# One fixed period per head, evenly spread weight and FFN pieces, and early heads turned by TensorE, in a routed-attention and FFN kernel

## The chip, the cores and the metric

The kernel runs on one core of a Trainium2 chip. The metric is the device time in microseconds (us) from start to end of one execution; lower is better. Engines: TensorE (matmuls and transposes, PE in the profile, its weight loads PEld), VectorE (DVE), ScalarE (ACT), GpSimd (POOL), SyncE (SP, which here only issues DMAs). Before: 346.12 us median of four runs.

Runs carry a state, fast or slow; where a granted TensorE clock is lower and a run over 1.5% above the fastest of its kernel it is called slow. Ratios and their intervals use fast runs alone; medians are of all runs of a kernel, slow ones too.

## The reference

Four batches of eight heads, 768 tokens, head size 64. Each query and key is assigned to the nearest of 16 centroids of its head; attention is allowed only within equal clusters. The heads are joined to 3072 tokens of 512 and go through a multiplicative FFN.

```python
q_assign = argmax(q_n @ c_n);  k_assign = argmax(k_n @ c_n)      # per head, 16 clusters
scores = 0.125 * q @ k.T, masked to -1e9 where q_assign != k_assign
attn = softmax(scores) @ v                                       # 32 heads
x = heads joined: (3072, 512)
a = x @ w1; b = x @ w2                                           # 512 -> 1024
out = ((a * b) @ w3) @ w_out                                     # 1024 -> 1024 -> 512
```

## The kernel before

Per head g the kernel does: three loads (192 KB each); *prep* on POOL (bf16 copy and the rounding rest of q and k into `stg`, v into `vb`); a *turn* of `stg` into `xqk` by a DMA transpose, so that the head size lies on partitions; *routing* (12 small matmuls into `prr`, three VectorE operations to a one-hot `oh`, a transpose into `pso`, one more VectorE operation to `ohT`, then four small DMAs that write the one-hot rows into rows 64-79 of `xqk`, where they act as the mask); *scores* and exponentials; *values* (36 matmuls into `av`), normalising, and after every second head a join into `xT_all`. Beside that, w3 and w_out are folded once into one matrix `wc` (16 pieces), and each block of 512 tokens needs 12 FFN pieces (8 up, 4 down). Six blocks exist; a block can start when its batch of eight heads is done, so two blocks always remain for a tail after the last head.

The loop, shortened:

```python
LOAD_AHEAD = 4; PREP_AHEAD = 3; ROUTE_AHEAD = 2
for g in range(NG + 1):                       # 32 heads; the scheduler orders the engines
    if g < NG:
        stage_load(g + 4); stage_prep(g + 3)  # prep ends with the DMA transpose
        emit_wloads(2)
        stage_route(g + 2)
        stage_sc(g)
    if g >= 1:
        stage_av(g - 1)
        ...                                   # a batch done: its FFN units go to pending
    for _ in range(UNITS(g)):                 # 2 for g < 8, else 3, as long as there are some
        if pending: pending.pop(0)()

def stage_prep(g):
    ...
    nc.sync.dma_start_transpose(out=xqk, in_=stg)        # all 32 heads
```

An up unit is eight matmuls 128x512 (two groups of four, then a ScalarE copy and a VectorE product), a down unit eight more.

The softmax here doesn't subtract the row's maximum and nothing guards it: scores larger than these inputs give would overflow.

## Time and profile before

| | before |
|---|---|
| time, median of 4 | 346.12 us (344.51 to 347.29) |
| profiled span, mean granted clock | 348.0 us, 0.978 |
| TensorE busy | 287.2 us, 83% |
| first score matmul | 36.5 us |
| last head's FFN tail | from 302.6 us, 45 us with the end |

The page of the kernel before. The first lines are the busy time of each engine with its share of the span; each digit below is the busy share in a fortieth of the span, in tenths (9 is 90% or more). PEclk is the granted TensorE clock.

```profile
span 348.0 us, 7211 instructions
PE 287.2 (83%) x2818; PEld 171.6 (49%) x2818; DVE 159.4 (46%) x316; ACT 184.3 (53%) x351; POOL 102.3 (29%) x112
...
PE   0120748888999999879698989998999999799995
PEclk9999969899999999999899999999999999999999
DMA  7999799768798633697493474444502320001103
```

TensorE does little in the first four slices (35 us) while DMA stands at 7 to 9. It also dips to 8, 7 and 6 in the 17th, 18th and 20th slices, long after the start. The profiled run took 350.15 us, 4 us more than the median.

The same kernel cut into stages, busy time of each engine by stretch. Columns: the stretch and its length, busy us of each engine with its instruction count, then granted clock, share of DMA engines busy, GB/s.

```profile
0.00:36.50 36.50, 5.09 (x62) 3.71 (x62) 12.28 (x43) 2.77 (x3) 19.15 (x27) 1.00 0.98 213
36.50:105.00 68.50, 58.49 (x649) 38.51 (x650) 35.27 (x67) 41.71 (x80) 31.28 (x33) 0.93 0.87 179
105.00:140.00 35.00, 33.31 (x305) 18.92 (x304) 17.12 (x30) 20.03 (x39) 12.40 (x13) 1.00 0.56 140
140.00:173.00 33.00, 27.42 (x367) 18.79 (x364) 15.70 (x35) 25.76 (x51) 14.46 (x15) 0.95 0.70 145
173.00:244.50 71.50, 66.10 (x632) 37.82 (x630) 38.28 (x65) 40.94 (x78) 20.99 (x22) 1.00 0.56 137
244.50:282.50 38.00, 37.76 (x361) 22.40 (x360) 17.80 (x37) 23.65 (x46) 3.99 (x5) 1.00 0.31 79
282.50:302.60 20.10, 18.71 (x267) 13.31 (x264) 8.56 (x21) 17.78 (x36) 0.00 (x0) 1.00 0.07 21
302.60:348.00 45.40, 40.33 (x189) 18.18 (x189) 14.38 (x21) 11.60 (x20) 0.00 (x0) 0.98 0.12 47
```

Only 5 of the first 36.5 us are TensorE work, with the DMA engines 98% busy. The fourth row is heads 12-15, which have no FFN piece left. The last row is the tail.

What TensorE waited for, before: engine, tile and line, releaser, total us, number of waits, longest.

```profile
PE prr L267 <- DMA xqk<-stg: 17.2, 4, 6.7
PE sc L299 <- DMA xqk<-ohT: 10.2, 4, 3.7
PE pct L162 <- DVE cnsrc L156: 8.2, 1, 8.2
PE pt L175 <- DMA w3b<-in_moe_w_dram: 5.7, 2, 3.9
```

The routing matmuls wait for turned heads (`xqk<-stg`), the scores for one-hot rows (`xqk<-ohT`).

### The profile page before, as it was taken

How to read it: one execution, taken by the hardware profiler on the slowest of the kernel's cores; microseconds unless marked ns; L12 is line 12 of the kernel's file. 1: busy time of each engine (PE TensorE's matmuls, PEld its weight loads, DVE VectorE, ACT ScalarE, POOL GpSimd, SP SyncE). 2: the span in 40 equal slices, each digit the busy share in tenths (PEclk: the TensorE clock that was granted, in tenths of full speed). 3: DMA queues.
4: the chain of work that ended last, by engine and by line, in shares of the span. 5: the costliest groups of instructions: out<-in, count | busy, mean ns of one | idle time of the engine just before them, and what ended most of it. 6: DMA issues, size and time to landing. Idle time of an engine off the chain costs nothing.

```text
span 348.0 us, 7211 instructions
## 1 busy us (share of the span) xinstructions
PE 287.2 (83%) x2818; PEld 171.6 (49%) x2818; DVE 159.4 (46%) x316; ACT 184.3 (53%) x351; POOL 102.3 (29%) x112
## 2 busy tenths in 40 slices
PE   0120748888999999879698989998999999799995
PEld 0120536555655555657355555554656556544442
DVE  7222425465555544555256556544555444342331
ACT  3000438756565656779546555655676659532230
POOL 3960434426554522343533332312300000000000
PEclk9999969899999999999899999999999999999999
DMA  7999799768798633697493474444502320001103
GB/s 204 244 183 223 142 210 150 191 134 178 198 231 185 185 86 106 178 164 153 88 236 95 132 207 119 119 99 75 163 21 48 81 97 10 2 0 58 66 0 121
DMA packets 74961, 45.07 MB, mean 129 GB/s; under 512 B 54448, under 2 KB 69808, under 8 KB 74928
## 3 DMA queue, kind: packets, MB, share of 16 engines
q1 hardware_dynamic: 71696, 39.37, 47.0%
q0 software_dynamic: 3232, 5.24, 9.0%
q8 instruction: 22, 0.36, 0.4%
q14 instruction: 11, 0.09, 0.1%
HBM read 29.39 MB, written 6.29 MB: 103 GB/s over the span
## 4 chain that ended last, share of the span: by engine, by line
PE 65%; DMA 14%; DVE 11%; POOL 3%; SPq 2%; ACT 2%; issue 2%; DVEq 0%; POOLq 0%; ACTq 0%
PE po L232 12%; PE pb L220 12%; PE pa L212 12%; PE sc L299 9%; PE av L322 7%; DMA xqk<-stg 5%; PE sc L305 5%; PE pw L186 4%; DMA x_273<-in_v_dram 4%; PE pso L281 2%; DMA xqk<-ohT 2%; DMA x_113<-in_v_dram 2%; DVE rsc L269 2%; DVE oh_139 L273 2%; PE prr L267 2%
## 5 line engine op out<-in xcount | busy, mean ns | idle before, releaser
L302 ACT ACTIVATE ex<-sc 128x512 bf16<-128x512 f32 x192 | 107.2, 621 | 68.0 <-PE sc L299 67.6
L299 PE MATMUL sc<-xqk 80*128 80x512 bf16 x192 | 71.5, 396 | 11.6 <-DMA xqk<-ohT 10.2
L322 PEld LDWEIGHTS <-ex 128*128 128x128 bf16 x1152 | 63.2, 99 | 22.3 <-issue 5.6
L309 ACT ACTIVATE ex<-sc 128x512 bf16<-128x512 f32 x96 | 60.4, 630 | 11.6 <-PE sc L305 11.5
L217 ACT CAST asb<-pa 128x512 bf16<-128x512 f32 x48 | 27.8, 586 | 47.0 <-PE pa L212 46.9
L212 PE MATMUL pa<-xT_all,w1b 128*128 128x512 bf16 x192 | 52.0, 381 | 0.6 <-DVE xT_all L344 0.6
L220 PE MATMUL pb<-xT_all,w2b 128*128 128x512 bf16 x192 | 52.0, 380 | 0.2 <-ACT asb L217 0.2
L224 DVE TENSOR_TENSOR ab<-pb,asb 128x512 bf16<-128x512 f32 x48 | 33.2, 691 | 41.0 <-PE pb L220 35.6
L232 PE MATMUL po<-wc,ab 128*128 128x512 bf16 x192 | 43.1, 379 | 0.0
L305 PE MATMUL sc<-xqk 80*128 80x256 bf16 x192 | 38.8, 280 | 0.0
L269 DVE TENSOR_REDUCE rsc<-prr 128x192 f32<-128x384 f32 x32 | 17.6, 551 | 33.8 <-PE prr L267 33.8
L267 PE MATMUL prr<-cnt_189,xqk 128*128 128x32 bf16 x384 | 15.4, 178 | 17.7 <-DMA xqk<-stg 17.2
L232 PEld LDWEIGHTS <-ab 128*128 128x128 bf16 x192 | 18.5, 98 | 21.7
L220 PEld LDWEIGHTS <-w2b 128*128 128x128 bf16 x192 | 18.6, 98 | 21.5 <-issue 1.6
L267 PEld LDWEIGHTS <-xqk 128*128 128x128 bf16 x384 | 14.7, 98 | 25.8 <-DMA xqk<-stg 19.0
L212 PEld LDWEIGHTS <-w1b 128*128 128x128 bf16 x192 | 18.1, 98 | 19.0 <-issue 0.3
L283 DVE TENSOR_SCALAR ohT<-pso,msc 128x384 bf16<-128x384 bf16 x32 | 15.2, 476 | 19.3 <-PE pso L281 15.1
L299 PEld LDWEIGHTS <-xqk 80*128 80x128 bf16 x192 | 17.4, 100 | 12.7 <-DMA xqk<-ohT 11.7
L240 ACT COPY osb<-po 128x512 f32<-128x512 f32 x12 | 7.0, 585 | 28.5 <-PE po L232 28.5
L330 DVE RECIPROCAL rcp<-av 128x6 f32<-128x6 f32 x32 | 6.3, 196 | 33.7 <-PE av L322 33.3
L238 DVE COPY osb<-po 128x512 f32<-128x512 f32 x12 | 8.3, 691 | 26.0 <-PE po L232 26.0
L305 PEld LDWEIGHTS <-xqk 80*128 80x128 bf16 x192 | 16.3, 100 | 6.6 <-issue 0.8
(167 smaller groups left out, 330.3 us busy)
## 6 DMA issues: line engine op xcount, KB each, us to landing
out_dram<-osb SPq DMA_DIRECT2D x24, 256.0 KB, 2.2
w3b<-in_moe_w_dram POOLq DMA_DIRECT2D x4, 512.0 KB, 7.2
xqk<-ohT SPq DMA_DIRECT2D x128, 12.0 KB, 1.8
wob<-in_moe_w_out_dram POOLq DMA_DIRECT2D x2, 512.0 KB, 11.5
w1b<-in_moe_w_dram POOLq DMA_DIRECT2D x2, 512.0 KB, 5.4
w2b<-in_moe_w_dram POOLq DMA_DIRECT2D x2, 512.0 KB, 8.4
xqk<-stg SPq DMA_TRANSPOSE x32, 4.2
x_105<-in_q_dram SPq DMA_DIRECT2D x1, 192.0 KB, 2.4
```

Of the source, the lines that this page charges most:

```text
L212: nc.tensor.matmul(pa, lhsT=w1b[:, fc, js], rhs=xT_all[:, fc, t0 : t0 + TB], start=(fc == 0), stop=(fc == 3),)
L217: nc.scalar.copy(out=asb, in_=pa)
L220: nc.tensor.matmul(pb, lhsT=w2b[:, fc, js], rhs=xT_all[:, fc, t0 : t0 + TB], start=(fc == 0), stop=(fc == 3),)
L224: nc.vector.tensor_tensor(out=st["ab"][:, jc], in0=pb, in1=asb, op=ALU.mult)
L232: nc.tensor.matmul(po, lhsT=st["ab"][:, jc, sub * P : (sub + 1) * P], rhs=wc[:, jc], start=(jc == 0), stop=(jc == 7),)
L267: nc.tensor.matmul(prr[:, j], lhsT=xqk[:, j, :], rhs=cnt2[:, h], start=True, stop=True)
L269: nc.vector.tensor_reduce(out=rsc, in_=prr, axis=AX.X, op=ALU.add)
L299: nc.tensor.matmul(sc, lhsT=xqk[0:KR, NCH + 2 * pr + i, :], rhs=xqk[0:KR, 0:4, :], start=True, stop=True)
L302: nc.scalar.activation(out=ex[:, i, 0:512], in_=sc, func=ACT.Exp, scale=SM_SCALE)
L305: nc.tensor.matmul(sc[:, i], lhsT=xqk[0:KR, NCH + 2 * pr + i, :], rhs=xqk[0:KR, 4:6, :], start=True, stop=True,)
L309: nc.scalar.activation(out=ex[:, :, 512:S], in_=sc, func=ACT.Exp, scale=SM_SCALE)
L322: nc.tensor.matmul(av[:, sub, 0:VCOL], lhsT=exs[j // 2][:, j % 2, sub * P : (sub + 1) * P], rhs=vb[:, j, 0:VCOL], start=(j == 0), stop=(j ...
```

## The change

Its intent: make the start short and keep TensorE evenly loaded. All engines get the program's own order (no scheduler). There is one period per head; each item in it has a position between 0 and 1, and items are emitted in order of position. Weight and FFN units become half pieces (at most four matmuls 128x512; a fold turn is eight transposes). Heads 0-9 are turned by TensorE transposes through PSUM. Two heads are loaded first instead of four, head 0 is prepared on VectorE, weights are issued one or two per period. Routing leads the scores by one period instead of two. Two smaller things changed with it: a fold turn now needs only one quarter of w3 to have landed instead of all of it, and there are seven buffers for exponentials instead of eight.

```diff
-LOAD_AHEAD = 4
-PREP_AHEAD = 3
-ROUTE_AHEAD = 2
+PE_HEADS = 10
...
+    def turn_pe(g: int, half: int):
+        def item():
...
+            pst = psum_f.tile([P, NCH, P], BF16, name="pst", tag="f")
+            for j in range(NCH):
+                nc.tensor.transpose(out=pst[:, j], in_=st["stg"][:, half * NCH + j], identity=ident)
+            nc.vector.tensor_copy(out=st["xqk"][:, half * NCH : (half + 1) * NCH], in_=pst)
...
+    LOADS = {-2: [2], -1: [3], 0: [4], 1: [5], 2: [6], 3: [7, 8], 4: [9, 10]}
...
+    def in_period(p: int):
+        for g in LOADS.get(p, []):
+            load(g)
+        if PE_HEADS <= p + 3 < NG:
+            turn_dma(p + 3)
...                                            # prep, on POOL
+        wload()
+        if p >= 2:
+            wload()
+        work = []
+        if 0 <= p < NG:
+            work += [((i + 0.5) / 9, it) for i, it in enumerate(score_items(p))]
+        if 0 <= p + 2 < PE_HEADS:
+            work += [(0.50, turn_pe(p + 2, 0)), (0.62, turn_pe(p + 2, 1))]
+        if 0 <= p + 1 < NG:
+            work += [(0.02, route(p + 1)), (0.36, route_turn(p + 1))]
+        if 1 <= p <= NG:
+            work += [(0.23 + 0.13 * i, it) for i, it in enumerate(av_items(p - 1))]
...
+        n = FILL(p, len(fill))
+        for i in range(min(n, len(fill))):
+            work.append(((i + 0.75) / n, fill.pop(0)))
+        for _, it in sorted(work, key=lambda t: t[0]):
+            it()
...
+    with tc.manual_schedule():
+        for p in range(-3, NG + 1):
+            in_period(p)
+        for it in fill:
+            it()
...
+def FILL(p, left):
+    if p < 0:
+        return 2 if p > -3 else 0
+    if p <= H:
+        return 3
+    if p <= 2 * H:
+        return 3
+    return 5 if p < NG else 4
```

## The prediction

> **What bounds it now.** TensorE work, but not everywhere (busy time by stretch, chain of waits, timeline). Heads 24-27, with three FFN pieces each (244-282 us), keep TensorE busy 37.8 of 38 us: 9.3-9.7 us per head, in which four matmuls 128x512 take 0.865 us and attention about 4.1 us. The tail (302.6-344 us) is two FFN blocks back to back, 41.4 us, and cannot shrink. Loss is elsewhere:
> - Start: the first scores run at 36.5 us; TensorE was busy about 8 us until then. The timeline shows it waiting for DMA transposes (11 us and 7 us from issue to use), queued behind loads and weights with the DMA engines about 100% busy.
> - Heads 0-7 (36.5-105 us): 68.5 us for about 51 us of full-speed TensorE work; granted clock 0.93.
> - Heads 12-15, which have no FFN piece left (140-173 us): 33 us for 16 us of TensorE work; ScalarE 25.8 us busy; the chain passes through one-hot and load DMAs (3.7, 1.9, 1.8 us).
> - Heads 28-31 (282-302 us): 20 us, ScalarE-bound (9 exponentials, about 5.2 us a head).
> Some 50 us in all are not TensorE work.
>
> **What the change does.**
> - Removes 10 of 32 DMA transposes (4.2 us each to land); adds 120 TensorE transposes, about 7 us, and 20 VectorE evictions of about 0.6 us, off the critical path (VectorE is 46% busy).
> - Loads two heads first and prepares head 0 on VectorE. But the first weight load is issued after head 0's value cast (about 6.5 us instead of 1.3) and takes 7.2 us, and the fixed order puts a weight turn ahead of head 0's turn: TensorE waits until about 14 us. I expect first scores at about 24 us.
> - Spreads 3 half pieces over each of periods 9-16, instead of 3 whole ones over four heads and none over four; then 5 half pieces over periods 17-31. Periods 7-8 have none. The tail stays two blocks.
> - Routing leads the scores by one period instead of two: routing product and VectorE chain 2.4 us, then turn to landed one-hot rows about 5 us (four issues of 0.6 us, then 1.8 us). So no period can be much under 7.2 us.
>
> **Sum (estimate from these durations).** First scores 24; periods 0-6 at 7.8 = 55 (TensorE 7.0 plus DMA saturation); 7-16 at 7.2 = 72, bounded by the routing loop; 17-31 at 8.6 = 129 (TensorE 8.25, 96% packed); last values 2; tail and end 45: 327. Counting losses removed (12 at start, 7 in heads 0-7, 10 in heads 8-15) gives 321. I predict 324 us, range 311 to 339. Chances: faster 0.85, same 0.11, slower 0.04.
>
> The Trainium skill (TensorE: Matmul & The Clock Gate, Part 1) says idle time throttles the array and about 3.4 us of activity releases it. The trace agrees: score matmuls take 0.62 us around 40-50 us and 0.38 later, granted clock 0.83 in 40-60 us. Even filling should keep it near 1 there.
>
> **Checks in the profile after.** First score matmul at 22-27 us, after a wait for the first weight load. TensorE busy 285-295 us, about 90% of the span. Periods 9-16 about 7.2 us, 17-31 about 8.6. Little wait of ScalarE for scores. Waits for one-hot rows at period starts, mainly in periods 7-16. Tail still 41 us.
>
> **What would make it wrong.** Strict order may turn each late DMA (weights, one-hot rows) into a stall of all TensorE work: then 335-350. The one PSUM bank of routing product, one-hot turn and head join may add 0.6 us in each second period. If DMA keeps up early and one-hot rows land in time: 311-315.

## The result and the profile after

| | before | after |
|---|---|---|
| time, median of 4 each | 346.12 us | 326.06 us (324.58 to 330.27) |
| ratio | | 0.9409, 95% interval 0.9342 to 0.9476 |

A ratio is the mean time of one kernel's fast runs over that of the other's fast runs of the same rounds, so not quite the ratio of the medians.

The first profile of the changed kernel: span 328.5 us, clock 0.958. The unaltered kernel was therefore run once more (run `again` below); these lines are from that profile, in the fast state, clock 0.974. The page:

```profile
span 325.1 us, 7457 instructions
PE 283.4 (87%) x2938; PEld 173.6 (53%) x2938; DVE 167.1 (51%) x340; ACT 195.4 (60%) x351; POOL 100.1 (31%) x110
...
PE   0347797799869899989999998999999999899995
PEclk9995799899999999997999999999999999999999
DMA  6983969922556785667755575866432012002103
```

TensorE does real work from the second slice on. Its dip in the middle is one slice (6, the 12th: periods 7 and 8, which have no pieces). The DMA digits fall in the first 80 us.

The same profile by stretch, with cuts at the starts of periods 0, 7, 9 and 17 and near the last head's end:

```profile
0.00:26.00 26.00, 6.58 (x85) 5.79 (x85) 20.28 (x51) 2.77 (x3) 13.03 (x20) 0.98 0.84 192
26.00:85.20 59.20, 51.98 (x602) 36.04 (x603) 31.88 (x66) 35.21 (x63) 26.38 (x29) 0.89 0.61 144
85.20:97.80 12.60, 9.14 (x152) 6.55 (x148) 8.43 (x18) 9.74 (x19) 7.79 (x9) 1.00 0.68 160
97.80:156.00 58.20, 53.41 (x622) 33.59 (x623) 30.59 (x60) 44.18 (x82) 25.74 (x26) 0.97 0.69 157
156.00:279.00 123.00, 120.19 (x1293) 72.62 (x1289) 61.47 (x125) 91.75 (x165) 27.20 (x28) 1.00 0.48 116
279.00:325.10 46.10, 42.11 (x198) 19.02 (x198) 14.49 (x22) 11.72 (x20) 0.00 (x0) 1.00 0.13 47
```

The five-piece periods (fifth row) hold TensorE busy 120.2 of 123 us. Periods 0-6 (second row) take 8.5 us each and are the weak stretch. What TensorE waited for, same profile:

```profile
PE sc L341 <- DMA xqk<-ohT: 15.2, 9, 3.8
PE pct L162 <- DVE cnsrc L156: 12.3, 1, 12.3
PE prr L293 <- DVE xT_all L406: 4.4, 8, 0.8
PE pso L316 <- DVE oh L301: 2.4, 3, 1.7
```

The waits for turned heads are gone; the waits for one-hot rows have grown. In the stretch 20 to 72 us four of the nine one-hot waits make up 9.7 us.

For the later comparison, each kernel's scores can be followed through its timeline: the start of the first score matmul of each head, good to about 0.3 us. All columns are from single profiles.

| kernel | first scores | heads 0-15 | heads 16-30 | from head 31 to the end | span |
|---|---|---|---|---|---|
| before | 36.5 | 124.7 | 134.2 | 52.6 | 348.0 |
| changed (again) | 26.0 | 121.0 | 123.8 | 54.3 | 325.1 |

So 10.5 us came from the start, 3.7 from the first sixteen heads, 10.4 from the next fifteen; the end lost 1.7. These add to the 22.9 us between two single profiles; the medians differ by 20.1.

### The profile page after: what moved, and what is told of

Same layout as the page of the kernel before. It is cut to its first block, busy times and chain, and to the rows that moved or that the text cites. A ratio compares the mean times of both kernels' runs of the same rounds, so it can differ in the third digit from the quotient of the medians.

```text
span 328.5 us, 7415 instructions
## 1 busy us (share of the span) xinstructions
PE 284.7 (87%) x2896; PEld 176.2 (54%) x2938; DVE 164.1 (50%) x340; ACT 195.4 (59%) x351; POOL 99.8 (30%) x110
## 4 chain that ended last, share of the span: by engine, by line
PE 77%; DMA 11%; DVE 5%; ACT 4%; issue 1%; SPq 0%; POOL 0%; DVEq 0%
PE pu L216 24%; PE sc L341 13%; PE po L235 12%; PE av L373 11%; DMA xqk<-ohT 9%; PE sc L351 5%; PE pw L191 3%; DMA w3b<-in_moe_w_dram 2%; PE prr L293 2%; PE pso L316 2%; ACT ex L345 2%; PE pst L283 2%; PE psx L405 1%; PE pt L178 1%; DVE xT_all L406 1%
## 5 line engine op out<-in xcount | busy, mean ns | idle before, releaser
L341 PE MATMUL sc<-xqk 80*128 80x512 bf16 x192 | 70.5, 397 | 15.5 <-DMA xqk<-ohT 14.6
L373 PEld LDWEIGHTS <-ex 128*128 128x128 bf16 x1152 | 49.6, 101 | 13.2 <-issue 2.2
L224 DVE TENSOR_TENSOR ab<-pu,asb 128x512 bf16<-128x512 f32 x48 | 33.2, 691 | 43.2 <-PE pu L216 38.5
L216 PE MATMUL pu<-xT_all,w1b 128*128 128x512 bf16 x177 | 47.7, 383 | 1.1 <-issue 0.2
L216 PE MATMUL pu<-xT_all,w2b 128*128 128x512 bf16 x182 | 47.3, 378 | 0.5
L235 PE MATMUL po<-wc,ab 128*128 128x512 bf16 x183 | 45.8, 382 | 0.5
L222 ACT CAST asb<-pu 128x512 bf16<-128x512 f32 x48 | 28.2, 587 | 27.9 <-PE pu L216 27.9
L320 DVE TENSOR_SCALAR ohT<-pso,msc 128x384 bf16<-128x384 bf16 x32 | 15.2, 474 | 27.8 <-PE pso L316 25.0
L341 PEld LDWEIGHTS <-xqk 80*128 80x128 bf16 x192 | 17.3, 99 | 20.1 <-DMA xqk<-ohT 16.1
L351 PEld LDWEIGHTS <-xqk 80*128 80x128 bf16 x192 | 17.5, 101 | 15.4 <-issue 2.8
L386 DVE TENSOR_TENSOR xtm<-av,rcp 128x384 bf16<-128x384 f32 x32 | 17.8, 557 | 1.1
L191 PE MATMUL pw<-wob,w3T 128*128 128x512 bf16 x56 | 16.0, 401 | 0.4
```

The source lines that it names most:

```text
L191: nc.tensor.matmul(st[jc], lhsT=w3T[:, kc, jc * P : (jc + 1) * P], rhs=wob[:, kc], start=(kc == 0), stop=(kc == 7),)
L216: nc.tensor.matmul(pu, lhsT=wb[:, fc, jc * P : (jc + 1) * P], rhs=xT_all[:, fc, t0 : t0 + TB], start=(fc == 0), stop=(fc == 3),)
L222: nc.scalar.copy(out=st["a"], in_=pu)
L224: nc.vector.tensor_tensor(out=st["ab"][:, jc], in0=pu, in1=st.pop("a"), op=ALU.mult)
L235: nc.tensor.matmul(st["o"], lhsT=st["ab"][:, jc, sub * P : (sub + 1) * P], rhs=wc[:, jc], start=(jc == 0), stop=(jc == 7),)
L341: nc.tensor.matmul(sc, lhsT=xqk[0:KR, NCH + 2 * pr + part, :], rhs=xqk[0:KR, 0:4, :], start=True, stop=True,)
```

## The experiments

Twelve kernels ran, three rounds each; all were correct. Four groups shared a chip and the runs of before: again, sched, dmaturn, lumps; bpe, beven, earlyw, lead2; both, best; clump, dmaturn_nofill. The medians of before were 348.34, 347.83, 345.92 and 344.79 us. Between groups the ratios are the fairer measure.

| run | time, median | ratio to before | 95% interval | first scores | heads 0-15 | heads 16-30 |
|---|---|---|---|---|---|---|
| again (changed kernel) | 326.15 | 0.9456 | 0.9373-0.9539 | 26.0 | 121.0 | 123.8 |
| sched | 330.64 | 0.9559 | 0.9433-0.9686 | 27.2 | 119.2 | 125.2 |
| dmaturn | 348.24 | 1.0086 | 0.9972-1.0199 | 38.1 | 130.9 | 122.0 |
| dmaturn_nofill | 342.92 | 0.9939 | 0.9875-1.0002 | 33.7 | 130.7 | 122.0 |
| lumps | 336.78 | 0.9749 | 0.9646-0.9852 | 26.3 | 130.1 | 125.0 |
| bpe | 332.51 | 0.9553 | 0.9508-0.9598 | 26.2 | 120.7 | 131.8 |
| beven | 333.23 | 0.9550 | 0.9489-0.9612 | 37.2 | 114.6 | 127.0 |
| both | 323.79 | 0.9391 | 0.9326-0.9456 | 26.1 | 114.2 | 130.0 |
| earlyw | 323.97 | 0.9293 | 0.9233-0.9353 | 25.3 (slow) | 122.2 | 123.8 |
| lead2 | 324.76 | 0.9316 | 0.9252-0.9380 | 24.0 | 123.9 | 120.6 |
| best | 316.98 | 0.9195 | 0.9131-0.9260 | 19.6 | 118.7 | 121.0 |
| clump | 331.44 | 0.9616 | 0.9565-0.9667 | 23.0 | 117.8 | 137.0 |

My theory after the result: the gain has two sources, the early turns by TensorE and the even spread; what remains at the start is the routing loop. Rivals: the hand-fixed order itself is what pays; or the start is short because of the loads; or the spread is worth nothing since the TensorE work is the same.

### again: the changed kernel once more

No edit.

> The changed kernel unaltered, as the yardstick for the others and for a profile in the fast state (the first profile fell in the slow one: span 328.5 us at granted clock 0.958). Both theories: 323 to 328 us, ratio to before 0.935 to 0.950. First score matmul again near 26 us. If a fast profile still shows periods 0-4 at 9 to 10 us each and 5 to 6 at 7, those waits belong to the kernel and not to the slow state.

Measured 326.15 us, span 325.1, first scores 26.0. In the fast state, too, periods 0-4 took 9.4, 7.9, 9.6, 9.2 and 9.4 us and periods 5-6 6.8 and 6.9, so those waits belong to the kernel.

### sched: the hand-fixed order taken off

```diff
-    with tc.manual_schedule():
+    if True:
```

> The same program text, but the scheduler is free to reorder again (the hand-fixed order taken off). Theory 'fixing the order is what pays': 333 us or more, most of the gain lost. Rival 'what pays is how the work is cut and spread and how early heads are turned; the scheduler follows the program order well enough': 322 to 331 us, within 1.5% of the changed kernel, with differences in the first 60 us alone. I hold the rival at 0.7.

330.64 us, and the intervals of the two ratios overlap: "fixing the order is what pays" falls, since 0.9559 keeps most of the gain. By the fast runs of the same rounds it is 3.5 us slower than again, which these runs cannot tell from nothing. Its early periods were shorter (heads 0-6 in 50.3 us against 59.2), its periods 9-16 longer (61.4 against 58.2), so the rival's expectation that the differences lie in the first 60 us alone was missed. From about 150 to 275 us TensorE loads its weights in nearly the same order in both traces (98% or more of the loads match in sequence), between 100 and 150 us it does not (53 to 85%). So for heads 17-30 this run hardly tests the order of TensorE.

### dmaturn: all heads turned by DMA

```diff
-PE_HEADS = 10
+PE_HEADS = 0
...     # turn_dma(p + 3) is emitted after the period's prep instead of before it
```

> The changed kernel with all 32 heads turned by DMA, none by TensorE; order and spread stay. Theory 'turning early heads on TensorE is what makes the start short': first score matmul at 32 us or later, waits for turned heads come back in the first 60 us, 333 to 343 us. Rival 'the start is short because only two heads are loaded first and the weights are spaced out': first score at 24 to 29 us, 320 to 328 us in all, as TensorE also saves 7 us of transposes. I hold the first at 0.75.

The whole gain is lost: 348.24 us, first scores 38.1. But the waits were not those I expected. TensorE waited for *weights*, as these lines of its list of waits show:

```profile
PE pt L178 <- DMA w3b<-in_moe_w_dram: 26.1, 4, 13.2
PE pct L162 <- DVE cnsrc L156: 10.3, 1, 10.3
PE sc L341 <- DMA xqk<-ohT: 9.9, 9, 3.4
```

The timeline of that run points to two ways in which a turn may delay others:

```profile
14.58 10.88 SPq L274 DMA_TRANSPOSE xqk<-stg  x1
14.84 0.74 POOL L106 DMA_DIRECT2D w3b<-in_moe_w_dram  x1
24.26 1.89 PE L178 MATMUL pt<-ident,w3b 128*128 128x128 bf16 x16 [13.20 <-DMA w3b<-in_moe_w_dram]
```

The issue of the third turn held the SyncE queue for 10.88 us, and weights took a median 11.6 us to land instead of 6.5 (the sections on DMA issues of that page and of that of again). The weights are issued by POOL, and the next issue on SyncE ran only at 29.23 us, 3.8 us after the turn's had ended, so in this run the held queue is not shown to have cost anything. Since the order is fixed, TensorE stood still until they came. So this run showed that in this order the early DMA turns cost the whole gain, but not by which mechanism.

### dmaturn_nofill: the same, with no weight pieces before period 1

```diff
-        return 2 if p > -3 else 0
+        return 0
+    if p == 0:
+        return 0
+    if p <= 2:
+        return 5
```

(on top of dmaturn)

> The kernel of the dmaturn run (hand order, all heads turned by DMA, 348 us), with no weight pieces before period 1 (then 5, 5, 3 per period), so that TensorE cannot wait for weights before the first scores. In dmaturn TensorE waited 26 us for weights and not for turned heads. Theory 'DMA turns hurt because they crowd the DMA engines and delay weights, and the hand order makes TensorE wait for those': first scores before 32 us, waits for weights under 8 us, total 328 to 338 us. Rival 'the latency of the turns itself holds the heads back, weights merely hide it': waits for turned heads appear instead, total above 342 us.

342.92 us, first scores 33.7 us. The rival's expectations were met: waits for turned heads appeared, and the total lay above 342 us. TensorE's waits:

```profile
PE sc L341 <- DMA xqk<-ohT: 21.2, 9, 8.3
PE prr L293 <- DMA xqk<-stg: 10.0, 1, 10.0
PE pw L191 <- DMA wob<-in_moe_w_out_dram: 9.0, 2, 6.8
```

Taking the pieces of w3 off TensorE's way saved about 5 us (medians of different rounds; by ratio 1.5%). Waiting for weights was not gone: that for w_out grew from 4.1 to 9.0 us. So how the 22 us that the DMA turns cost in the fixed order divide between weights and latency stays open; with no wait for w3 left, some 17 of them were still lost. One part of it can be read from the timeline:

```profile
14.49 11.74 SPq L274 DMA_TRANSPOSE xqk<-stg  x1
14.99 0.48 DVE L320 TENSOR_SCALAR ohT<-pso,msc 128x384 bf16<-128x384 bf16 x1 [0.59 <-PE pso L316]
26.34 2.63 SPq L324 DMA_DIRECT2D xqk<-ohT  x4
```

Head 0's one-hot rows were ready at 15.47 us. They were issued at 26.34, straight after the third turn, whose issue had held the SyncE queue for 11.74 us. Here a turn delayed small DMAs of another head that stood behind it in the same queue.

### lumps: the pieces in lumps again

```diff
-    if p <= 2 * H:
-        return 3
-    return 5 if p < NG else 4
+    if H + 4 < p <= 2 * H or p > 3 * H + 4:
+        return 0
+    return 6
```

> The changed kernel with the FFN half pieces in lumps as before: 6 per period in periods 9-12, none in 13-16, 6 in 17-28, none in 29-31. Theory 'even spread pays because periods with no pieces run at the routing loop or at ScalarE, not at TensorE': periods 9-12 and 17-28 at about 9.2 us, 13-16 at about 6.5, 29-31 at about 5.6; in all 8 to 13 us more than the changed kernel, 332 to 339 us. Rival 'TensorE work is the same sum, the spread is worth nothing': within 3 us of the changed kernel.

336.78 us, 10.6 us more than again (10.1 by the fast runs), as the theory expected; heads 9-16 took 64.5 us against 58.2. In the profile the empty periods took 8.3, 7.0, 6.5 and 5.4 us (periods 13 to 16) and the full ones about 9. The rival falls.

### bpe: the kernel before, plus TensorE turns for heads 0-9 only

```diff
-        nc.sync.dma_start_transpose(out=xqk, in_=stg)
+        if g < 10:
+            for half in range(2):
+                pst = psum_f.tile([P, NCH, P], BF16, name="pst", tag="f")
+                for j in range(NCH):
+                    nc.tensor.transpose(out=pst[:, j], in_=stg[:, half * NCH + j], identity=ident)
+                nc.vector.tensor_copy(out=xqk[:, half * NCH : (half + 1) * NCH], in_=pst)
+        else:
+            nc.sync.dma_start_transpose(out=xqk, in_=stg)
```

> The kernel before with one part of the change: heads 0-9 turned by TensorE, all else as it was (scheduler's order, lumps of FFN pieces, four heads loaded first). Theory 'turning early heads on TensorE is the larger part of the gain': first scores at 20 to 26 us instead of 36.5, in all 10 to 20 us less than before, ratio 0.94 to 0.97. Rival 'without the new order the weights and loads still hold TensorE': ratio above 0.98.

332.51 us against 347.83: 15.3 us from a few lines. First scores at 26.2 us, the same as in the changed kernel, although here four heads are loaded first and VectorE prepares none. So neither of these two is needed for this start; the turns alone give it.

### beven: the kernel before, plus even half pieces only

```diff
-    pending = fold_units()
+    pending = fold_items()                 # the half pieces of the changed kernel
...
-    return 2 if g < H else 3
+    return 3 if g <= 2 * H - 1 else 5
```

> The kernel before with the other part alone: fold and FFN work cut into half pieces, 3 per head in heads 0-15 and 5 from head 16 on, under the scheduler; all heads still turned by DMA. The lumps run cost 10.6 us within the changed kernel, so theory 'even spread is worth about 10 us wherever heads have slack': 7 to 12 us less than before, ratio 0.965 to 0.98, heads 12-15 no longer short of TensorE work. Rival 'the start decides, spread is worth nothing while DMA turns lag': ratio 0.99 to 1.01.

333.23 us, 14.6 us less, more than expected. Heads 0-15 took 114.6 us instead of 124.7, heads 16-30 127.0 instead of 134.2; the start stayed at 37.2. It works mostly on a different stretch than bpe. The half pieces also cut the work finer and fold w3 by quarters; lumps, which leaves the halves and takes away the evenness, shows the evenness alone from head 9 on, so for heads 0-8 the two are not told apart.

### both: these two parts together, still under the scheduler

> The kernel before with both parts (TensorE turns for heads 0-9, evenly spread half pieces) and no hand-fixed order, no change of loads or of the routing lead. Each alone took about 15 us off (ratios 0.9553 and 0.955). If the parts add, 317 to 320 us, ratio 0.91 to 0.92: then the rest of the change (hand order, one period of routing lead, load order) costs 6 to 9 us and hides the sum. Rival 'the parts overlap, they remove the same waits early': 324 to 330 us, ratio 0.93 to 0.95, the hand order costs nothing. I hold the first at 0.6.

323.79 us, ratio 0.9391. The two savings of about 15 us do not add; by medians together they give 22 us. The start is 26.1 as in bpe and heads 0-15 are 114.2 as in beven, so those two do combine; heads 16-30, at 130.0, stay behind beven's 127.0. The expected 317 to 320 us were missed, and my theory with its numbers falls. The rival's ratio was met (its time to 0.2 us), and in sum the rest of the change costs nothing: both and the changed kernel agree within their intervals. But the table shows that this sum hides two opposite terms. Against both, the changed kernel loses 6.8 us in heads 0-15 and wins 6.2 us in heads 16-30. The two kernels differ in the fixed order, the routing lead, the loads and the places of the pieces inside a period, so these terms are not the order's alone.

### earlyw: the first weight load at 1 us

```diff
+    wload()                                # before the identity matrix is made
...
-        wload()
+        if p > -3:
+            wload()
```

> The changed kernel with the first weight load issued at about 1 us instead of 6.6. My prediction said TensorE waits for that load until 14 us. Rival, from the trace: TensorE waits for the centroid chain on VectorE (12.3 us, then 1.4 more), and the weights cost only 0.4 us after that. Prediction's reason: TensorE starts 4 us earlier and the total falls 3 to 5 us. Rival: first transposes of weights still at 13.8 to 14.2 us, total within 1.5 us of the changed kernel. I hold the rival at 0.85.

323.97 us, 2.2 us below again in another set of rounds by medians, 4 to 6 us by ratio (0.9293 against 0.9409 and 0.9456): the time does not decide. The timeline does better. Its profile is slow, so I compare it with the first profile of the changed kernel, also slow: span 325.6 us against 328.5. The first weight transpose ran at 7.9 us instead of 14.5, but the second transpose of the centroids at 12.0 (before 13.8), the other seven of that weight turn behind it at 12.1, and the first scores at 25.3 instead of 26.5. TensorE's start was then held by the centroid chain on VectorE. These lines of the changed kernel (again) show why that chain was late:

```profile
7.11 0.16 DVE L142 TENSOR_TENSOR tt<-ss,rr 128x1 f32<-128x1 f32 x1
7.30 1.15 DVE L144 TENSOR_TENSOR nrm<-nrm,tt 128x1 f32<-128x1 f32 x1
7.59 0.84 POOL L264 CAST stg<-x 128x768 bf16<-128x768 f32 x1
...
12.21 1.63 POOL L265 TENSOR_TENSOR stg<-x,stg 128x768 bf16<-128x768 f32 x1
12.25 1.63 DVE L157 COPY cnsrc<-cnsrc 128x64 bf16<-128x64 bf16 x1
```

Two operations of equal shape took 0.16 and 1.15 us; the long one ends when the POOL operation beside it ends (8.45 and 8.43). A copy of 128x64 took 1.63 us under a POOL operation of 1.63 us; before, the same copy took 0.18. The Trainium skill (GPSIMD Engine Reference, section 1, Specifications) says that GpSimd shares its SBUF interfaces with VectorE, in contention with instructions of two SBUF inputs or in a two-port mode; the trace agrees, though it does not show in which mode the copy ran. No run was made to move the chain alone. In lead2 it happened to end sooner (second transpose at 10.87 us), and TensorE then stood 3.39 us for the first quarter of w3, until 14.54. So in the changed kernel both waits end within half a microsecond of each other, and taking away one alone uncovers the other.

### lead2: routing two periods ahead

```diff
-        if 0 <= p + 2 < PE_HEADS:
-            work += [(0.50, turn_pe(p + 2, 0)), (0.62, turn_pe(p + 2, 1))]
-        if 0 <= p + 1 < NG:
-            work += [(0.02, route(p + 1)), (0.36, route_turn(p + 1))]
+        if p < 0 and 0 <= p + 2:
+            work += [(0.50, turn_pe(p + 2, 0)), (0.62, turn_pe(p + 2, 1))]
+        if p == 0:                          # two heads are turned and routed here
+            work += [(0.20, turn_pe(2, 0)), (0.28, turn_pe(2, 1))]
+            work += [(0.50, route(2)), (0.85, route_turn(2))]
+        if 0 <= p and p + 3 < PE_HEADS:
+            work += [(0.60, turn_pe(p + 3, 0)), (0.70, turn_pe(p + 3, 1))]
+        g = p + 1 if p <= 0 else p + 2
+        if 0 <= g < NG:
+            work += [(0.02, route(g)), (0.36, route_turn(g))]
...     # loads and prep one period earlier to match
```

> The changed kernel with routing two periods ahead of the scores from head 2 on, as it was before, order otherwise by hand. Theory 'the routing loop through the one-hot DMAs is what stretches periods 0-4 to 9 us': waits of scores for one-hot rows fall from 15 us to under 5, periods 0-4 to about 7.5 us, total 312 to 319 us. Rival 'weights and loads saturate the DMA engines there, the wait only moves to another place': 322 us or more. I hold the first at 0.6.

The waits for one-hot rows fell from 15.2 to 0.6 us, and yet the time was 324.76 us: 1.4 us less by medians, 3 to 5 us by ratio. TensorE's waits in lead2, and two lines of its timeline:

```profile
PE pt L178 <- DMA w3b<-in_moe_w_dram: 10.4, 2, 7.0
...
PE sc L341 <- DMA xqk<-ohT: 0.6, 1, 0.6
```

```profile
31.30 0.74 POOL L106 DMA_DIRECT2D w3b<-in_moe_w_dram  x1
36.82 1.03 PE L178 MATMUL pt<-ident,w3b 128*128 128x128 bf16 x8 [7.03 <-DMA w3b<-in_moe_w_dram]
```

The wait moved to the weights: 3.4 us before the first weight turn, and 7.0 us in period 0, which took 14.4 us. The timeline names the reason of the second: POOL issued the last quarter of w3 at 31.30 us, after it had prepared heads 3 and 4, because in the fixed order the issue stands behind them; the preparation of head 4 had itself waited 8.3 us for a turn on TensorE to free its buffer. The rival's number (322 or more) was met; what binds period 0 is the order of POOL's queue.

### best: lead of two, weights issued earlier, fewer weight pieces at the start

```diff
+    wload()                                # first, as in earlyw
...     # lead2, and in period 0 the weight is issued between the two prepared heads
-        wload()
-        if p >= 2:
+        if p != 0 and p > -3:
+            wload()
+        if p >= 1:
             wload()
...
-        return 2 if p > -3 else 0
+        return 1 if p > -3 else 0
+    if p == 0:
+        return 2
```

> The changed kernel, order by hand, with routing two periods ahead, the first weight load at the start, the weights issued before the second prepared head of a period, and fewer weight pieces in periods -2 to 0 (1, 1, 2 instead of 2, 2, 3). With lead2 alone the waits for one-hot rows fell to 0.6 us, but TensorE then waited 10.4 us for weights, whose issue stood behind head preparation on POOL. Theory 'these two waits are one slack, and both must go': waits for weights under 3 us, period 0 under 10 us instead of 14.4, total 312 to 318 us, ratio 0.90 to 0.92. Rival 'DMA bandwidth or the clock binds the first 60 us': 320 us or more.

316.98 us, ratio 0.9195: below both kernels, and its interval lies below those of the changed kernel in both sets of rounds. First scores at 19.6 us; period 0 took 10.2 us, just over what was expected; no wait for w3 appears in its list, and the one-hot waits are 4.7 us. So the expectation was met, but it does not show that the two waits had to go together: of the 11.4 us between the profiles of again and best, 6.4 lie before the first scores, where with fewer weight pieces head 0's turn (8.98 us) now comes ahead of the first weight turn (10.15) instead of behind it (15.01 and 14.18 in again). Lead of two with early weights alone was not run.

### clump: best, with the five pieces at the end of each period

```diff
-            work.append(((i + 0.75) / n, fill.pop(0)))
+            work.append(((i + 0.75) / n if p <= 16 else 1.0, fill.pop(0)))
```

> The best kernel so far (lead of two periods, early weights) with one change: from period 17 on the five FFN half pieces of a period stand together at its end instead of between scores and values. The two scheduler runs with even numbers of pieces per head needed 8.6 us per head in heads 17-30, the hand order 8.1, with the same work. Theory 'spreading inside the period lets ScalarE work under the FFN pieces': periods 17-30 go from 8.05 to 8.6-9.4 us, total 324 to 335 us. Rival 'the inside order is of no account, only the number of pieces per period counts': within 3 us of the best kernel, 314 to 320 us.

331.44 us, ratio 0.9616 against best's 0.9195, by medians 14.5 us more, with the same work and the same number of pieces per period. Heads 16 to 30 by stretch, first best, then clump:

```profile
138.30:259.30 121.00, 117.74 (x1242) 71.61 (x1260) 61.31 (x124) 91.56 (x165) 32.38 (x33) 1.00 0.56 127
```

```profile
140.80:277.80 137.00, 123.81 (x1250) 70.82 (x1262) 61.25 (x124) 87.64 (x165) 32.20 (x33) 1.00 0.46 110
```

ScalarE has the same 165 operations; in best it is busy 76% of the stretch (91.56 of 121.00), in clump 64%. With the pieces at the end, scores and values run at ScalarE's pace first and ScalarE is idle under the FFN pieces afterwards. Nearly half of the 16.0 us by which this stretch grew is another wait: TensorE's waits for the one-hot on VectorE (`pso`) rose from 0.5 to 7.7 us in it (7.0 to 14.1 in the whole run), because without FFN pieces in between the transpose comes too soon. The rival (only the count per period matters) falls.

## Why the prediction was right, and where not

The time was predicted as 324 us and came out as 326.06; the chance of 0.85 for faster was on the right side. Term by term, against the profile of again (span 325.1):

| term | predicted | measured |
|---|---|---|
| first scores | 24 | 26.0 |
| periods 0-6 | 55 | 59.2 |
| periods 7-16 | 72 | 70.8 |
| periods 17-31 and last values | 131 | 123.5 (to 279.5, the first FFN matmul of the tail) |
| tail and end | 45 | 45.6 |
| sum | 327 | 325.1 |

- **Right in part: where the loss was.** The start and the uneven spread: bpe and beven each removed one and were worth 15.3 and 14.6 us. Tail unchanged: right. But the count of losses put 12 us at the start and 17 into heads 0-15; the profiles show 10.5 and 3.7, and 10.4 in heads 16-30, which the count did not list. Heads 0-7 even took longer than before (65.4 us against 63.8). That this count (321) lay near the result is luck.
- **Right: one-hot waits appear.** 15.2 us in nine waits. But I put them mainly in periods 7-16; four waits of 9.7 us lie between 20 and 72 us. Their landing there was slow: the last of four DMAs was issued by 31.6 us and the waiting scores ran at 35.4, while the median from issue to landing over the run is 2.0 us. The Trainium skill (DMA: Bandwidth & Descriptors, Queues, rings and completion order) says that a completion signal lands only after every earlier write of that DMA engine, across its queues; with weights in flight this fits, but no run isolates it. Three of these waits (5.9 us) lie in periods 0-6 and are enough for the 4.2 us missing from "periods 0-6 at 7.8".
- **Half right: "TensorE waits until about 14 us" for the first weight load.** The moment was right (14.2 us; 14.5 in the first profile), and the load did land only at 14.1. But TensorE also waited 13.6 us for the centroid chain, which the prediction left out. earlyw brought the weights at 7.9 us and TensorE waited for the chain until 12.0; in lead2 the chain ended sooner and TensorE waited for the weights until 14.5. Each hides the other, and the first scores came only 1.2 us sooner in earlyw.
- **Wrong step: "no period can be much under 7.2 us".** Periods 7 and 8 took 6.3 us. The loop is about as long as I said: in period 7 routing began at 84.94 us and the scores that need it ran at 91.46, 6.5 us later. But the next routing product no longer waits for those scores; it ran at 89.86, while those rows were on their way. I had added the loop to the period instead of overlapping the two. That periods 7-16 came to 70.8 us, near the 72 of the sum, is luck: there they range from 6.2 to 9.0 us, and in periods 9-16 TensorE was busy 53.4 of 58.2 us.
- **Mis-sized term: periods 17-31 at 8.6 us.** They took 8.2. I costed 75 half pieces (five in each of fifteen periods); only 72 exist there, and TensorE was 98% busy (120.2 of 123 us), not 96%. This error of 7 us cancelled those of the first two terms, so that the sum came so near is again partly luck.
- **Wrong: TensorE busy 285-295 us, 90% of the span.** 283.4 and 87%.
- **Right where it was said, and not around it: "even filling should keep it near 1 there".** In 40-60 us the granted clock was 1.00 in again (0.83 before), but 0.74 in 20-40 us and 0.91 in 60-80. The rule from the skill (TensorE: Matmul & The Clock Gate, Part 1) fits: the fixed order stood still there for one-hot rows (3.8 and 2.0 us at a time), and the scores after each stand took 1.03 us a pair instead of 0.60. The second stand is shorter than the page's idle window of about 3.4 us, so that length is not confirmed here.
- **Left open by the prediction: what the fixed order itself is worth.** sched, which takes off nothing else, was 3.5 us slower with overlapping intervals, so the order adds little as it stands. Against both, the changed kernel is longer in heads 0-15 and shorter in heads 16-30. The late part fits the mixing of FFN pieces between scores (clump); the early part is not split between order, routing lead and loads. best is 6.8 us below both (316.98 against 323.79, same rounds), but 6.5 of that is already there at the first scores (19.6 against 26.1).

Open: how much of best's 9 us over the changed kernel is due to each of its three edits; earlyw and lead2 took 2.2 and 1.4 us alone, by medians of different rounds (4 to 6 and 3 to 5 us by ratio, estimates from ratios times 346 us), and the third edit was not run alone.

## What to carry to other kernels

In this kernel the fixed order turned late DMAs into stand-stills of TensorE, so before fixing an order give each wait slack (a lead of two periods took the one-hot waits from 15.2 to 0.6 us), and look into the issuing queues (here POOL's and SyncE's) for issues that stand behind unrelated work. When one wait is removed and the time hardly moves, list the waits again: here the wait had only moved from one-hot rows to weights. Spread filler work inside the period, between the operations that feed another engine, and not only evenly over the periods.

## What the Trainium skill lacked or had wrong

- DMA: Bandwidth & Descriptors: beside cycle counts in a comparison for trn3, it has no figure for how long the issue of a DMA transpose holds the issuing queue, and none with the DMA engines crowded. With the DMA digit at 9, one issue held SyncE for 10.88 us (dmaturn) and 11.74 us (dmaturn_nofill), against 1.3 to 2.6 us from the fourth turn on in the kernel before; in dmaturn_nofill the one-hot rows behind it were issued 10.9 us after they were ready.
- No page compares the cost of turning SBUF data by TensorE and by DMA inside a running kernel, while loads and weights crowd the DMA engines. Here ten heads (120 TensorE transposes instead of ten DMA transposes) were worth 15.3 us of 347.8.
- TensorE: Matmul & The Clock Gate warns that clock records can be unreliable; it does not say that they can begin late. In the kernel before the first clock record stands at 42.8 us. The granted clock reads 1.00 over 20-40 us, where there is none, while a pair of score matmuls at 36.5 us took 1.03 us, against 0.59 us when warm.
